# Attention into two feed-forward layers into routed experts: a two-byte search product and reshaped sums in the routing search, one product in place of two in the late second layer, and new step delays

## Chip, cores and metric

One core of one Trainium2 chip runs the whole program. The metric is the device time of one execution in microseconds. The engines are PE (matrix products), PEld (its weight loads), DVE and POOL (elementwise work and reductions; POOL also issues the indirect transfers), ACT (copies and activations) and SP (transfers). "Product" below means one matrix instruction on PE.

## What is computed

The reference, cut down:

```python
# attention over 32 memory slots per head: 8 batches, 8 heads, 576 positions, width 64
x = attn_out.transpose(0, 2, 1, 3).reshape(4608, 512)
# first feed-forward part: d_model 512, d_ff 768
h = np.maximum(np.maximum(x @ w1, x @ w2), x @ w3)
x = h @ w_out
# routed experts: 8 experts, cap = 4608 / 8 = 576 tokens each
logits = x @ w_gate
for idx in np.argsort(-logits.flatten()):      # greedy: best pair (token, expert) first
    tok, e = idx // 8, idx % 8
    if assigned[tok] >= 0 or counts[e] >= cap: continue
    assigned[tok] = e; counts[e] += 1
out[assigned == e] = np.maximum(x[assigned == e] @ w1[e], 0) @ w2[e]   # for each e
```

All inputs are float32, and the kernel keeps nearly full accuracy: each large product is done as three products of split operands (high by high, high by low, low by high).

## The kernel before, in words

The tokens are worked in four units of two batches (u = 0 to 3), nine tiles of 128 tokens each. For a unit the kernel does the attention, folds its result into the weights of the first layer (`fold`), runs the first layer (`layer1`, products of 288 columns) and the second (`layer2`). `layer2` makes 512 outputs and 8 gate logits at once: `w_out` has the product `w_out @ w_gate` set behind it as columns 512 to 519 (tiles `woh`, `wol`), so that a tile of 128 tokens takes 6 x 3 pairs of products of 260 columns. For the last two units the gate logits come ahead of the second layer, by `last_logits` (products of the whole hidden layer with the small matrix `wpp`, collected in `sc`, then `last_logits2`: copy, transposes, copy to `L`), and the last 15 of the 18 second-layer tiles of these units run after all logits are known. They are the first cover of the routing search.

The greedy assignment is done in eight phases (`ph`), one expert becoming full in each. A phase is a search for the threshold at which an expert is full, over the bits of the float, with 3 or 31 candidates at a time:

- `choose`: each token's best open expert (`OH`, 128 x 36 x 8) and its value `me`; then `reach` (which candidates each token reaches).
- seven rounds of `count` (nine products of `reach` with `OH` on PE, then five small DVE instructions that end in `some`) and `digit` (one product of `some` with `number` on PE that broadcasts the digit found, then DVE makes the next candidates `kj` and the next `reach`).
- after the last digit `cuts`: how many tokens of each expert lie above the threshold and at it, per partition (`part`).
- `close`: a product sums `part` over the partitions; DVE finds the expert that is full and updates the state. `ties` and `places` each start with a product of `before` with `lastb`; `places2` (four times) builds selection matrices `P1`, and `index` (36 products) turns them into the token list `gi`, `si` of the expert.

POOL then gathers the 576 token rows (`xg`, five indirect transfers), PE transposes them (`tr`, L974), and the expert runs its first layer (`l1`, 192 products of 288 columns) and its second (`l2`, 96 products of 512 columns for four tiles and 16 for the last 64 tokens). POOL splits the next expert's weights into low parts meanwhile (`al`, L985; `bl`, L995), and scatters the results.

The order of all this on the in-order engines is fixed when the program is written out. `Flow` keeps a queue of search steps, each with a delay; `flow.main` writes out a unit of main work (three or so products) and first pops queued steps that are due. The delay of a step is how much main work, in planned microseconds, stands between it and the next step. If a step's input is not ready when PE comes to its product, PE waits and everything behind waits too. Just before the fourth tile of `l2` (tile index t = 3) `ready(ph+1)` pops, without main work between, whatever is still queued up to the next token list, and issues its gather.

Of the kernel before, what the change touches and what calls it, by code (L numbers as in the profile page):

```python
# [142 lines left out]
def moe_kernel(tc, q, k, v, phi, w1, w2, w3, w_out, w_gate, m_w1, m_w2, out):  # L143
# [16 lines left out]
    with ExitStack() as ctx:  # L160
# [487 lines left out]
        def layer2(u, t, c, j):  # L648
            if c == 0 and j == 0:
                st["ps"] = [pp.tile([128, NA], F32, name="acc", bufs=3),  # L650
                            pp.tile([128, NA], F32, **(dict(name="fold", bufs=2) if t % 2 else dict(name="acc", bufs=3)))]
            ps = st["ps"]
            n = hs.index((u, t, c)) + 2
# [12 lines left out]
            if i < NF - 1:  # L666
                return
            xs = wp.tile([128, DM], F32, name="xs", bufs=2)
            A.activation(xs[:, :NA], ps[0], AF.Copy)
            A.activation(xs[:, NA:], ps[1][:, :DM - NA], AF.Copy)  # L670
            if u < NU - 2:
                V.tensor_copy(L[:, u * NT + t], ps[1][:, DM - NA:])
            (SP if u >= NU - 2 else A).dma_start(x2s[u * TU + t * 128:u * TU + t * 128 + 128, :], xs)

        def last_logits(u, i):

            if i == 0:
                st["ll", u] = pp.tile([128, TU // 3], F32, name="sc", bufs=1)
            for c in range(3):
                PE.matmul(st["ll", u][32 * c:32 * c + E], wpp[:, i],  # L680
                          st["hT", u][:, i, TU // 3 * c:TU // 3 * (c + 1)], start=(i == 0), stop=(i == NF - 1))

        def last_logits2(u):
            ll = st["ll", u]
            x = wp.tile([128, DM], F32, name="xs", bufs=2)[:, :TU // 3]
            V.memset(x, 0.0)
            for c in range(3):
                A.activation(x[32 * c:32 * c + E], ll[32 * c:32 * c + E], AF.Copy)
            p = pp.tile([128, 3, 128], F32, name="tr", bufs=2)
# [14 lines left out]
        def choose(ph):  # L704

            src = L if ph == 0 else Lm
            if ph:
                ecap = small([128, E], "ecap")
                V.tensor_scalar(ecap, st["oh", ph - 1], -2.0, 1.0, op0=OP.mult, op1=OP.add)
                V.tensor_scalar(ecap, ecap, FMAX, None, op0=OP.mult)  # L710
                V.tensor_tensor(Lm, L if ph == 1 else Lm, br(ecap, NC), op=OP.min)
                src = Lm
                V.tensor_scalar(ucap, asg, 0.0, None, op0=OP.is_ge)
                V.tensor_scalar(ucap, ucap, -2.0, 1.0, op0=OP.mult, op1=OP.add)
                V.tensor_scalar(ucap, ucap, FMAX, None, op0=OP.mult)
# [3 lines left out]
            eq = small([128, NC, E], "eq", bufs=1)  # L719
            V.tensor_tensor(eq, src, bc(m, E), op=OP.is_equal)  # L720
            V.tensor_tensor(eq, eq, br(em8, NC), op=OP.mult)
# [12 lines left out]
        def search_steps(ph, DD):  # L734
# [18 lines left out]
            def digit(n):  # L753
# [3 lines left out]
                PE.matmul(p, some.to_broadcast([32, 128]), number[:, 1 - nj // J:2 - nj // J], start=True, stop=True)  # L757
# [51 lines left out]
        def finish_steps(ph, DD):  # L809
            last = ph == E - 1  # L810

            def close():
# [10 lines left out]
                else:  # L823
# [12 lines left out]
                    st["oh", ph] = oh  # L836
# [14 lines left out]

                    V.scalar_tensor_tensor(remR, oh, 1e6, remR, op0=OP.mult, op1=OP.add)
# [31 lines left out]
            def places():  # L884
# [10 lines left out]
                V.tensor_scalar(hi, pi, 7, None, op0=OP.arith_shift_right)  # L895
                eh = small([128, NC, 5], "eh", bufs=1)
# [4 lines left out]
                st["P1"] = lo, R, []  # L901
# [153 lines left out]
        def main1(u, i, n, w):  # L1055
            last = u == NU - 1
            layer1(u, i, n // 2, n % 2, w)
            at = (0, 6)
            if u and 3 * n + w in at and i + 1 < NF:
                fold(u, i + 1, at.index(3 * n + w))  # L1060
            if last and w == 1 and n == 1 and i:
                last_logits(u, i - 1)
            if not last and i == NF - 1 and n > 1 and w == 0:
                split_h(*hs[u * NT * NF // 3 + n - 2])


        before = onesb = row = lanef = vals = em8 = me8 = thr0 = rowi = OH = reach = some = number = part = remR = asg = ucap = sign = zero = Lm = am8 = me = rp = None

        def consts():
            nonlocal before, onesb, row, lanef, vals, em8, me8, thr0, rowi, OH, reach, some, number, part, remR, asg, ucap, sign, zero, Lm, am8, me, rp  # L1070
# [12 lines left out]
            later.G.iota(row, pattern=[[1, 128]], base=0, channel_multiplier=0, allow_small_or_imprecise_dtypes=True)  # L1083
            rowi = rp.tile([128, J], I32, name="rowi")
# [30 lines left out]
            later.V.tensor_scalar(em8, row[:, :E], -float(E), None, op0=OP.add)  # L1115
            me8 = rp.tile([128, E], F32, name="me8")
# [9 lines left out]
            some = rp.tile([32, 1], F32, name="some")  # L1126
            later.V.memset(some, 1.0)

            number = rp.tile([32, 2], F32, name="number")
            big = rp.tile([32, 1], F32, name="big")  # L1130
            later.V.tensor_scalar(big, lanef[:32], float(J), 2.0 ** 23, op0=OP.is_equal, op1=OP.mult)
            for n, x in enumerate((J, 3)):
                later.V.scalar_tensor_tensor(number[:, n:n + 1], lanef[:32], float(x), big, op0=OP.is_lt, op1=OP.add)
# [17 lines left out]
        for u in range(NU):  # L1151
# [50 lines left out]
            if u == NU - 2:  # L1202
                attention.close()
                hp = pool("last", side="right")
                for i in range(NF):
                    last_logits(u, i)
                last_logits2(u)
# [4 lines left out]
        for ph in range(E):  # L1212
            DD = DELAYS[SETS[ph]]
# [14 lines left out]
        flow.early()  # L1228
        flow.due = flow.now
        spacer = rp.tile([1, 1], F32, name="spacer")  # L1230
        for u, t, c in hs[((NU - 2) * NT + 3) * NF // 3:]:
            for j in range(3):
                flow.main(lambda: layer2(u, t, c, j), 0.67)
# [67 lines left out]
```

## Time and profile before

| | |
|---|---|
| three timed runs | 1162.79, 1162.80, 1165.26 us (median 1162.8) |
| profiled execution | 1156.12 us, of which the span from first to last instruction is 1154.3 us |
| busy share of the span | PE 92%, PEld 81%, DVE 63%, ACT 34%, POOL 29% |
| mean granted clock of PE | 0.977 |

Products on PE are pipelined: the duration of one is longer than the step from one start to the next, so the rate is read from start to start.

### The profile page before, as it was taken

What the parts mean: (1) busy time and instruction counts of PE and PEld (TensorE: products, weight loads), DVE (VectorE), ACT (ScalarE), POOL (GpSimd) and SP (SyncE); (2) the same over time, 40 slices, a digit from 0 to 9 for tenths busy, and PEclk for the clock granted to TensorE, in tenths of its full rate; (3) what the DMA queues carried; (4) which work ended last, traced back from release to release, by engine and by line L of the source; (5) the groups of instructions that cost most, each with busy time, mean ns of one, the idle gap of its engine ahead of it and who ended that gap; (6) DMA issues with size and microseconds to landing.
All of it is one profiled execution on the core that took longest, in us unless ns stands there. A gap on an engine that the chain in (4) does not pass through costs nothing.

```text
span 1154.3 us, 22040 instructions
## 1 busy us (share of the span) xinstructions
PE 1067.4 (92%) x8743; PEld 931.2 (81%) x8743; DVE 721.9 (63%) x1767; ACT 398.0 (34%) x897; POOL 338.2 (29%) x362
## 2 busy tenths in 40 slices
PE   4698999989999999999997899898999999899996
PEld 3577799878998889778997788778788887879895
DVE  6798843774646446344686577879787887862120
ACT  2454434433343243322332313324142332424240
POOL 2123210120101101000001444555544455556552
PEclk8899999999999999999998989999999999999999
DMA  9964535336322430210132232333313232334311
GB/s 286 324 199 141 183 115 167 108 96 199 104 83 70 138 97 24 74 42 1 47 128 69 83 106 87 110 101 111 114 61 112 82 118 92 121 104 128 106 55 41
DMA packets 103767, 127.80 MB, mean 111 GB/s; under 512 B 18928, under 2 KB 79344, under 8 KB 103664
## 3 DMA queue, kind: packets, MB, share of 16 engines
q1 hardware_dynamic: 95184, 102.80, 28.9%
q0 software_dynamic: 5888, 18.88, 5.2%
q10 hardware_dynamic: 2592, 4.72, 1.1%
q8 instruction: 69, 1.13, 0.4%
q14 instruction: 34, 0.28, 0.1%
HBM read 102.78 MB, written 23.59 MB: 109 GB/s over the span
## 4 chain that ended last, share of the span: by engine, by line
PE 43%; DVE 10%; issue 3%; POOL 2%; ACT 1%; DMA 0%; POOLq 0%
PE acc L1033 13%; PE acc L1010 12%; PE acc L602 5%; PE acc L664 4%; PE acc L1037 2%; PE tr L974 1%; DVE reach L731 1%; PE fold L757 1%; DVE eq L798 1%; PE fold L664 1%; DVE hT L1013 1%; PE fold L743 1%; DVE part L800 1%; POOL bl L995 1%; DVE kn L787 1%
## 5 line engine op out<-in xcount | busy, mean ns | idle before, releaser
L602 PE MATMUL acc<-ah,Wh 128*128 128x288 f32 x576 | 180.1, 313 | 4.9 <-DVE hT L608 3.6
L602 PE MATMUL acc<-ah,Wl 128*128 128x288 f32 x576 | 169.8, 295 | 1.2 <-DVE Wl L586 1.2
L602 PE MATMUL acc<-al,Wh 128*128 128x288 f32 x576 | 169.9, 295 | 0.0
L1033 PE MATMUL acc<-bh,hT 128*128 128x512 f32 x512 | 168.4, 399 | 0.0
L1010 PE MATMUL acc<-woh,ah 128*128 128x288 f32 x512 | 161.0, 314 | 1.7 <-ACT woh L976 1.2
L1010 PE MATMUL acc<-wol,ah 128*128 128x288 f32 x512 | 154.9, 303 | 0.2
L1010 PE MATMUL acc<-woh,al 128*128 128x288 f32 x512 | 154.1, 301 | 0.0
L602 PEld LDWEIGHTS acc<-ah,Wh 128*128 128x128 f32 x576 | 108.2, 188 | 33.3 <-issue 13.9
L608 DVE TENSOR_TENSOR hT<-hT,acc 128x288 f32<-128x288 f32 x192 | 85.9, 450 | 75.1 <-PE acc L602 69.0
L1033 PEld LDWEIGHTS acc<-bh,hT 128*128 128x128 f32 x512 | 96.1, 188 | 21.3
L602 PEld LDWEIGHTS acc<-ah,Wl 128*128 128x128 f32 x576 | 108.2, 188 | 1.4 <-DVE Wl L586 1.4
L602 PEld LDWEIGHTS acc<-al,Wh 128*128 128x128 f32 x576 | 108.4, 188 | 0.1
L985 POOL TENSOR_TENSOR al<-wa,ah 128x512 fp32r<-128x512 f32 x64 | 82.8, 1300 | 72.4 <-ACT ah L984 72.0
L1010 PEld LDWEIGHTS acc<-woh,ah 128*128 128x128 f32 x512 | 99.6, 195 | 3.2 <-ACT woh L976 1.7
L1012 ACT ACTIVATE hT<-acc 128x288 fp32r<-128x288 f32 x128 | 52.6, 411 | 142.4 <-PE acc L1010 136.4
L1033 PE MATMUL acc<-bl,hT 128*128 128x512 f32 x256 | 100.5, 392 | 0.0
L1010 PEld LDWEIGHTS acc<-wol,ah 128*128 128x128 f32 x512 | 99.5, 194 | 1.0 <-DVE wol L977 0.7
L1010 PEld LDWEIGHTS acc<-woh,al 128*128 128x128 f32 x512 | 99.6, 195 | 0.0
L962 POOL DMA_INDIRECT xg<-x2s,gi x40 | 39.3, 982 | 191.9 <-DVE some L751 172.7
L995 POOL TENSOR_TENSOR bl<-wa,bh 128x512 fp32r<-128x512 f32 x64 | 83.6, 1322 | 24.3 <-ACT bh L994 24.0
L1013 DVE SCALAR_TENSOR_TENSOR hT<-acc,hT 128x288 fp32r<-128x288 f32 x128 | 56.2, 452 | 52.4 <-ACT hT L1012 51.7
L606 ACT ACTIVATE hT<-acc 128x288 f32<-128x288 f32 x96 | 38.9, 411 | 144.6 <-PE acc L602 142.6
(253 smaller groups left out, 2204.9 us busy)
## 6 DMA issues: line engine op xcount, KB each, us to landing
wa<-in_moe_w_dram SPq DMA_DIRECT2D x64, 512.0 KB, 3.7
wr<-ws SPq DMA_DIRECT2D x36, 384.0 KB, 3.1
dw<-in_moe_w_dram SPq DMA_DIRECT2D x36, 256.0 KB, 5.3
q<-in_q_dram SPq DMA_DIRECT2D x7, 1024.0 KB, 5.9
kv<-in_k_dram SPq DMA_DIRECT2D x27, 256.0 KB, 4.1
kv<-in_v_dram SPq DMA_DIRECT2D x27, 256.0 KB, 4.9
ws<-wr SPq DMA_DIRECT2D x12, 384.0 KB, 3.1
x2s<-xs ACTq DMA_DIRECT2D x18, 256.0 KB, 2.0
```

The costliest lines, as they stand in the source:

```text
L602: PE.matmul(p, x[:, b, g, f], y[:, g, c], start=(n == 0), stop=(n == 5))
L606: A.activation(o, p, AF.Copy)
L608: V.tensor_tensor(o, o, p, op=OP.max)
L664: PE.matmul(ps[a], x[:, j], y[:, i, NA * a:NA * a + NA], start=(i == 0 and m == 0), stop=(i == NF - 1 and m == 2))
L962: G.indirect_dma_start(out=x[:n], out_offset=None, in_=x2s, in_offset=bass.IndirectOffsetOnAxis(ap=gi[:n, t:t + 1], axis=0))
L985: G.tensor_tensor(lo, r, hi.bitcast(F32), op=OP.subtract)
L995: G.tensor_tensor(lo, r, hi.bitcast(F32), op=OP.subtract)
L1010: PE.matmul(p, x[:, k], y[:, k, c], start=(k == 0 and i == 0), stop=(k == 3 and i == 2))
L1012: A.activation(hh[:, m, c], p, AF.Relu)
L1013: V.scalar_tensor_tensor(hl[:, m, c], p, 0.0, hh[:, m, c].bitcast(F32), op0=OP.max, op1=OP.subtract)
L1033: PE.matmul(p, x[:, m, c], y[:, m], start=(m == 0 and i == 0), stop=(m == K - 1 and i == 2))
L1037: PE.matmul(p, st["hx", m // 4][:, m % 4], y[:, m], start=(m == 0 and y is bh), stop=(m == K - 1 and y is bl))
```

## The change

It does eight things. (1) The digit's product takes two-byte operands and swaps their places: `number`, widened to 32 x 128 in bf16, becomes the loaded weight, and `some`, now bf16, the moving column. (2) `cuts` makes the signed flags `gs` in bf16, each doubled (last axis of 2, from `me` and the threshold at once), multiplies them with `OH` in bf16 into one tile `gx` for both thresholds, and sums that in one reduction; the float flags `ge` are made behind it. (3) `P1` is built from a doubled bf16 list `lod` and a bf16 row `rowb`. (4) `choose` uses a bf16 `em8b`; `ecap` is computed in `close` of the phase before, and `ucap` in two instructions in place of three. (5) `layer2` of the last two units drops the gate columns: one product of 512 columns in place of two of 260, one PSUM tile and one copy. (6) The logits of unit 2 are taken group by group inside unit 3's first layer, and collected in a `tr` tile. (7) The transposes of unit 3's logits come behind the first third of a late tile. (8) One set of delays replaces the two used in turn.

```diff
-DELAYS = ((4.38, 1.21, 1.9, 2.85, 3.39, 2.06, 2.18, 1.4, 1.31),
-          (3.53, 1.14, 2.24, 3, 3.11, 2.54, 2.15, 1.3, 1.62),
-          (3.33, 0.04, 2.75, 3.0, 3.09, 1.99, 2.38, 1.18, 1.41))
-SETS = (1, 0, 1, 0, 1, 0, 1, 0)
+DELAYS = (4.0, 1.3, 2.25, 4.2, 3.2, 3.5, 2.15, 0.9, 1.3)
...
-                for a in range(2):
-                    PE.matmul(ps[a], x[:, j], y[:, i, NA * a:NA * a + NA],
+                for a, p in enumerate(ps):
+                    PE.matmul(p, x[:, j], y[:, i, width * a:width * a + width],
...
-                PE.matmul(p, some.to_broadcast([32, 128]), number[:, 1 - nj // J:2 - nj // J], start=True, stop=True)
+                PE.matmul(p, number[:, 1 - nj // J], some, start=True, stop=True)
...
             def cuts(ph, t):
+                gs = small([128, 2, NC, 2], "gs", BF, bufs=1)
+                for j, op in enumerate((OP.is_gt, OP.is_ge)):
+                    V.scalar_tensor_tensor(gs[:, j], bc(me, 2), t, bc(sign, 2), op0=op, op1=OP.mult)
+                x = small([128, 2, NC, E], "gx", BF, bufs=1)
+                for j in range(2):
+                    V.tensor_tensor(x[:, j].rearrange("p c (k a) -> p c k a", a=2),
+                                    OH.rearrange("p c (k a) -> p c k a", a=2),
+                                    gs[:, j].unsqueeze(2).to_broadcast([128, NC, E // 2, 2]), op=OP.mult)
+                with nc.allow_low_precision("counts up to 36"):
+                    V.tensor_reduce(part, x.rearrange("p j c e -> p j e c"), axis=AX.X, op=OP.add)
                 ge = small([128, 2, NC], "ge", bufs=1)
                 V.tensor_scalar(ge[:, 0], me, t, None, op0=OP.is_gt)
                 V.tensor_scalar(ge[:, 1], me, t, None, op0=OP.is_ge)
-                gs = small([128, 2, NC], "gs", bufs=1)
-                V.tensor_tensor(gs, ge, br(sign, 2), op=OP.mult)
-                x = small([128, NC, E], "eq", bufs=1)
-                for j in range(2):
-                    V.tensor_tensor(x, OH, bc(gs[:, j], E), op=OP.mult)
-                    with nc.allow_low_precision("counts up to 36"):
-                        V.tensor_reduce(part[:, j], x.rearrange("p c e -> p e c"), axis=AX.X, op=OP.add)
...
-                V.tensor_tensor(x, bc(lo[:, NC // 4 * n:NC // 4 * (n + 1)], 128), br(row, NC // 4), op=OP.is_equal)
+                V.tensor_tensor(x.rearrange("p c (k a) -> p c k a", a=2),
+                                lo[:, NC // 4 * n:NC // 4 * (n + 1)].unsqueeze(2).to_broadcast([128, NC // 4, 64, 2]),
+                                rowb.rearrange("p (k a) -> p k a", a=2).unsqueeze(1).to_broadcast([128, NC // 4, 64, 2]),
+                                op=OP.is_equal)
...
+            if last and w == 1:
+                if n == 1 and i:
+                    last_logits(u, i - 1)
+                if n == 3 and i + 1 < NF:
+                    last_logits(u - 1, i)
...
+        for j in range(3):
+            layer2(*late[0], j)
+        last_logits3(NU - 1)
```

Three places show how the rows on the engines change. First PE in a late second-layer tile, around one digit of the first search phase (`acc` and `fold` are PSUM tiles, `hh` and `hl` the split hidden layer); before:

```order
L664 MATMUL acc<-woh,hh 128x260
L664 MATMUL fold<-woh,hh 128x260
L664 MATMUL acc<-wol,hh 128x260
L664 MATMUL fold<-wol,hh 128x260
L664 MATMUL acc<-woh,hl 128x260
L664 MATMUL fold<-woh,hl 128x260
L757 MATMUL fold<-number,some 128x1
L664 MATMUL acc<-woh,hh 128x260
```

And the same place now:

```order
L666 MATMUL acc<-woh,hh 128x512
L666 MATMUL acc<-wol,hh 128x512
L666 MATMUL acc<-woh,hl 128x512
L759 LDWEIGHTS number
L759 MATMUL fold<-some,number 128x1
L666 MATMUL acc<-woh,hh 128x512
```

Six products became three wider ones, and the digit has a weight load of its own that does not depend on `some`.

Second DVE, from the last digit of the second search phase to the start of its `close` (`hT` is the expert's hidden layer, not part of the search); before:

```order
L776 TENSOR_TENSOR fb<-fold,fbx 128x1
L792 TENSOR_SCALAR ge<-me,fb 128x36
L793 TENSOR_SCALAR ge<-me,fb 128x36
L795 TENSOR_TENSOR gs<-ge,sign 128x72
L798 TENSOR_TENSOR eq<-OH,gs 128x288
L800 TENSOR_REDUCE part<-eq 128x8
L798 TENSOR_TENSOR eq<-OH,gs 128x288
L800 TENSOR_REDUCE part<-eq 128x8
L1013 SCALAR_TENSOR_TENSOR hT<-acc,hT 128x288 x3
L828 TENSOR_TENSOR full<-fold,remR 128x8
```

And now:

```order
L778 TENSOR_TENSOR fb<-fold,fbx 128x1
L796 SCALAR_TENSOR_TENSOR gs<-me,fb,sign 128x72 x2
L799 TENSOR_TENSOR gx<-OH,gs 128x288 x2
L803 TENSOR_REDUCE part<-gx 128x16
L805 TENSOR_SCALAR ge<-me,fb 128x36
L806 TENSOR_SCALAR ge<-me,fb 128x36
L1027 SCALAR_TENSOR_TENSOR hT<-acc,hT 128x288 x2
L834 TENSOR_TENSOR full<-fold,remR 128x8
```

Five instructions stand between `fb` and the end of `part` where seven stood, and the two `ge` moved behind it.

Third POOL, in the first expert's second layer, from its first scatter (`out_dram`) to the next expert's first weight splits; before:

```order
L1044 MEMSET spacer 1x1
L1045 DMA out_dram<-o,si 4608x512
L1020 COPY xs<-hT 128x4x64 x2
L962 DMA xg<-x2s,gi 128x512 x4
L962 DMA xg<-x2s,gi 64x512
L1044 MEMSET spacer 1x1
L1045 DMA out_dram<-o,si 4608x512
L1020 COPY xs<-hT 128x4x64 x2
L1044 MEMSET spacer 1x1
L1045 DMA out_dram<-o,si 4608x512
L985 TENSOR_TENSOR al<-wa,ah 128x512 x2
```

And now:

```order
L1058 MEMSET spacer 1x1
L1059 DMA out_dram<-o,si 4608x512
L1034 COPY xs<-hT 128x4x64 x2
L1058 MEMSET spacer 1x1
L1059 DMA out_dram<-o,si 4608x512
L1034 COPY xs<-hT 128x4x64 x2
L1058 MEMSET spacer 1x1
L1059 DMA out_dram<-o,si 4608x512
L976 DMA xg<-x2s,gi 128x512 x4
L976 DMA xg<-x2s,gi 64x512
L999 TENSOR_TENSOR al<-wa,ah 128x512 x2
```

The gather of the next expert's tokens stood behind the first scatter and now stands behind the third, directly ahead of the splits.

## Rows read from the trace of the kernel before

**Rows 1.** Page: span and busy time by engine.

```profile
span 1154.3 us, 22040 instructions
...
PE 1067.4 (92%) x8743; PEld 931.2 (81%) x8743; DVE 721.9 (63%) x1767; ACT 398.0 (34%) x897; POOL 338.2 (29%) x362
```

**Rows 2.** Chain that ended last: start us, us, engine, tile and line, products.

```profile
599.42 4.45 PE acc L664 x37
...
665.54 6.74 PE acc L1010 x30
...
774.46 1.19 PE acc L1010 x9
...
865.60 4.98 PE acc L1010 x24
...
932.78 5.62 PE acc L1010 x30
...
974.73 0.80 PE acc L1010 x6
...
1038.68 25.56 PE acc L1010 x192
1064.24 22.19 PE acc L1033 x96
...
1092.86 11.92 PE acc L1010 x90
```

**Rows 3.** Waits of PE, 634 to 1040 us: who for whom, us, times, longest.

```profile
PE fold L825 <- DVE part L800: 15.4, 6, 4.4
PE fold L887 <- DVE lastb L879: 4.5, 4, 1.3
```

**Rows 4.** PE timeline around a digit (L757) and a `ties` product (L860).

```profile
711.00 0.29 PE L1010 MATMUL acc<-woh,al 128*128 128x288 f32 x1
711.23 0.38 PE L757 MATMUL fold<-number,some 32*128 32x1 f32 x2
...
711.77 0.30 PE L1010 MATMUL acc<-wol,ah 128*128 128x288 f32 x1
...
737.12 0.30 PE L1010 MATMUL acc<-woh,al 128*128 128x288 f32 x1
737.25 0.18 PE L860 MATMUL fold<-lastb,before 128*128 128x1 bf16 x1
...
737.50 0.30 PE L1010 MATMUL acc<-wol,ah 128*128 128x288 f32 x1
```

**Rows 5.** DVE timeline, first and last instruction of `cuts`, second phase.

```profile
727.87 1.20 DVE L792 TENSOR_SCALAR ge<-me,fb 128x36 f32<-128x36 f32 x1
...
732.45 0.67 DVE L800 TENSOR_REDUCE part<-eq 128x8 bf16<-128x288 f32 x1
```

**Rows 6.** DVE timeline, the same two instructions, first phase.

```profile
586.89 0.24 DVE L792 TENSOR_SCALAR ge<-me,fb 128x36 f32<-128x36 f32 x1
...
589.34 0.74 DVE L800 TENSOR_REDUCE part<-eq 128x8 bf16<-128x288 f32 x1
```

**Rows 7.** POOL timeline over the start of rows 5.

```profile
726.49 2.54 POOL L995 TENSOR_TENSOR bl<-wa,bh 128x512 fp32r<-128x512 f32 x2
```

**Rows 8.** Window after a wait: us, busy of PE, PEld, DVE, ACT, POOL, granted clock, DMA.

```profile
665.40:670.40 5.00, 5.00 (x22) 5.00 (x23) 3.29 (x20) 0.93 (x2) 1.28 (x1) 0.50 0.29 92
```

**Rows 9.** PE timeline at the last logits of units 2 and 3.

```profile
473.28 0.47 PE L691 MATMUL tr<-ident,xs 96*128 96x96 f32 x3 [1.62 <-ACT xs L688]
...
548.75 0.47 PE L691 MATMUL tr<-ident,xs 96*128 96x96 f32 x3 [1.55 <-ACT xs L688]
```

**Rows 10.** DVE group of `P1`: busy us, mean ns, idle before.

```profile
L906 DVE TENSOR_TENSOR P<-lo,row 128x1152 bf16<-128x1152 int32 x32 | 41.8, 1362 | 0.0
```

**Rows 11.** Page: gather's issue (busy us, mean ns) and us to landing.

```profile
L962 POOL DMA_INDIRECT xg<-x2s,gi x40 | 39.3, 982 | 191.9 <-DVE some L751 172.7
...
xg<-x2s,gi POOLq DMA_INDIRECT x40, 3.6
```

More of the change, by code (lines that the diff above doesn't have):

```diff
@@ L648, in layer2 @@
         def layer2(u, t, c, j):
+            late = u >= NU - 2
             if c == 0 and j == 0:
-                st["ps"] = [pp.tile([128, NA], F32, name="acc", bufs=3),
-                            pp.tile([128, NA], F32, **(dict(name="fold", bufs=2) if t % 2 else dict(name="acc", bufs=3)))]
+                if late:
+                    st["ps"] = [pp.tile([128, DM], F32, name="acc", bufs=3)]
+                else:
+                    st["ps"] = [pp.tile([128, NA], F32, name="acc", bufs=3),
+                                pp.tile([128, NA], F32, **(dict(name="fold", bufs=2) if t % 2 else dict(name="acc", bufs=3)))]
             ps = st["ps"]
+            width = DM if late else NA
             n = hs.index((u, t, c)) + 2
@@ L707, in choose @@
             if ph:
[L708 to L711, printed above, removed]
+                V.tensor_tensor(Lm, L if ph == 1 else Lm, br(st["ecap", ph - 1], NC), op=OP.min)
                 src = Lm
-                V.tensor_scalar(ucap, asg, 0.0, None, op0=OP.is_ge)
-                V.tensor_scalar(ucap, ucap, -2.0, 1.0, op0=OP.mult, op1=OP.add)
-                V.tensor_scalar(ucap, ucap, FMAX, None, op0=OP.mult)
+                V.tensor_scalar(ucap, asg, 0.0, -2.0, op0=OP.is_ge, op1=OP.mult)
+                V.tensor_scalar(ucap, ucap, 1.0, FMAX, op0=OP.add, op1=OP.mult)
             m = small([128, NC], "m")
@@ L718, in choose @@
             V.tensor_tensor(me, m, ucap, op=OP.min)
[L719 removed]
+            eq = small([128, NC, E], "eq", BF, bufs=1)
             V.tensor_tensor(eq, src, bc(m, E), op=OP.is_equal)
[L721 removed]
+            V.tensor_tensor(eq, eq, br(em8b, NC), op=OP.mult)
             V.tensor_reduce(am8, eq, axis=AX.X, op=OP.min)
@@ L850, in close @@
                     st["tie"] = tie, sc, lb, kk, amE, es
+                    ecap = st["ecap", ph] = small([128, E], "ecap")
+                    V.tensor_scalar(ecap, oh, -2.0, 1.0, op0=OP.mult, op1=OP.add)
+                    V.tensor_scalar(ecap, ecap, FMAX, None, op0=OP.mult)
                     V.scalar_tensor_tensor(remR, oh, 1e6, remR, op0=OP.mult, op1=OP.add)
@@ L1060, in main1 @@
                 fold(u, i + 1, at.index(3 * n + w))
-            if last and w == 1 and n == 1 and i:
-                last_logits(u, i - 1)
+            if last and w == 1:
[3 more added lines that the diff above has]
+                    last_logits(u - 1, i)
+                if i + 1 == NF and n in (0, 2, 3):
+                    (lambda u: last_logits(u, NF - 1), None, last_logits2, last_logits3)[n](u - 1)
             if not last and i == NF - 1 and n > 1 and w == 0:
                 split_h(*hs[u * NT * NF // 3 + n - 2])
-        before = onesb = row = lanef = vals = em8 = me8 = thr0 = rowi = OH = reach = some = number = part = remR = asg = ucap = sign = zero = Lm = am8 = me = rp = None
+        before = onesb = row = rowb = lanef = vals = em8 = em8b = me8 = thr0 = rowi = OH = reach = some = number = part = remR = asg = ucap = sign = zero = Lm = am8 = me = rp = None
         def consts():
-            nonlocal before, onesb, row, lanef, vals, em8, me8, thr0, rowi, OH, reach, some, number, part, remR, asg, ucap, sign, zero, Lm, am8, me, rp
+            nonlocal before, onesb, row, rowb, lanef, vals, em8, em8b, me8, thr0, rowi, OH, reach, some, number, part, remR, asg, ucap, sign, zero, Lm, am8, me, rp
             unit0.close()
@@ L1083, in consts @@
             later.G.iota(row, pattern=[[1, 128]], base=0, channel_multiplier=0, allow_small_or_imprecise_dtypes=True)
+            rowb = rp.tile([128, 128], BF, name="rowb")
+            later.V.tensor_copy(rowb, row)
             rowi = rp.tile([128, J], I32, name="rowi")
@@ L1115, in consts @@
             later.V.tensor_scalar(em8, row[:, :E], -float(E), None, op0=OP.add)
+            em8b = rp.tile([128, E], BF, name="em8b")
+            later.V.tensor_copy(em8b, em8)
             me8 = rp.tile([128, E], F32, name="me8")
@@ L1125, in consts @@
             later.V.memset(reach, 0.0)
-            some = rp.tile([32, 1], F32, name="some")
+            some = rp.tile([32, 1], BF, name="some")
             later.V.memset(some, 1.0)
-            number = rp.tile([32, 2], F32, name="number")
+            number = rp.tile([32, 2, 128], BF, name="number")
             big = rp.tile([32, 1], F32, name="big")
@@ L1132, in consts @@
             for n, x in enumerate((J, 3)):
-                later.V.scalar_tensor_tensor(number[:, n:n + 1], lanef[:32], float(x), big, op0=OP.is_lt, op1=OP.add)
+                later.V.scalar_tensor_tensor(number[:, n], lanef[:32].to_broadcast([32, 128]), float(x),
+                                             big.to_broadcast([32, 128]), op0=OP.is_lt, op1=OP.add)
             part = rp.tile([128, 2, E], BF, name="part")
@@ L1228, in moe_kernel @@
         flow.early()
+        spacer = rp.tile([1, 1], F32, name="spacer")
+        late = hs[((NU - 2) * NT + 3) * NF // 3:]
+        for j in range(3):
+            layer2(*late[0], j)
+        last_logits3(NU - 1)
         flow.due = flow.now
-        spacer = rp.tile([1, 1], F32, name="spacer")
-        for u, t, c in hs[((NU - 2) * NT + 3) * NF // 3:]:
+        for u, t, c in late[1:]:
             for j in range(3):
```

23 lines of the change are left out of this document (12 added, 11 removed).

## The prediction

> **What bounds the kernel now.** I read the page first: PE is busy 92% of the 1154.3 us span [rows 1], so a saving counts only if it shortens PE's own row of products or a wait in it. Then I followed the chain that ended last. From the seventh expert on it is PE alone: that expert has no search beside it, and takes from 1038.68 to 1092.86, 54.2 us [rows 2]. Experts three to five, with a search each, start at 774.46 and the sixth starts at 974.73: 66.8 us apiece [rows 2]. So a search costs an expert 12.6 us though PE's search products are tiny. Last I read PE's waits over the six experts with a search: 15.4 us in six waits for `part` at the `close` product, and 4.5 us in four for `lastb` at the `places` product [rows 3]. The rest is PE work of the search: digits above all (below).
>
> **Change by parts, against the profiled execution.**
>
> *Digit.* From the start of the product ahead to that of the second product behind, a digit takes 711.77 - 711.00 = 0.77 us; `ties`, which has the form the digit gets (two-byte operands, one moving column), takes 737.50 - 737.12 = 0.38 between like neighbours [rows 4]. Without inserted work two products of 288 columns take 2 x 0.133 (25.56 / 192 [rows 2]) = 0.27. So a digit falls from 0.50 to 0.11 or 0.12. There are 7 in each of 7 searches: 49 x 0.38 = **-18.6 us**. It is on PE's path in all of them but the two or three between the late layer and the first gather. Bounds: 0, if `some` ended last at every digit (PE mostly comes to it without a wait: the digit of rows 4 shows none), and -24, if the weight load, which no longer waits, also shortens the waits there are.
>
> *Cuts and their delay.* In the second phase `cuts` runs from 727.87 to 733.12, 5.25 us [rows 5]; in the first, where POOL is idle, from 586.89 to 590.08, 3.19 us [rows 6]. The difference is DVE being held: the first `ge` takes 1.20 us against 0.24, and ends at 729.07 where POOL's instruction ends at 729.03 [rows 5, 6, 7]. The new chain has two `gs`, two `gx`, one reduction of 576 elements. Estimates from rows: `gs` like `ge`, 0.24 each; `gx` at most half of a 1.36 us `P1` row scaled by 288 / 1152 plus a fixed 0.15, so 0.3 to 0.46; the reduction at most twice 0.74 [rows 6, 10]. Sum 2.6 to 2.9 us free of POOL. PE's cover between the last digit and `close` was 24 to 27 products of 288 columns (3.2 to 3.6 us); counted in the new order it is 15 of 288 and 12 of 512 columns in phases three to seven, 15 x 0.133 + 12 x 0.231 (22.19 / 96) = 4.8 us [rows 2], 21 and 9 in the second. One hold of 1 us is then covered, two nearly. Half of it lies in `l2`, where POOL splits nothing for the first three tiles. I leave 0.25 us a phase: **-14 us** of the 15.4 [rows 3], bounds -4 (as many holds as now) and -15.4.
>
> *What the wait does to the clock.* After the longest wait, five microseconds ran at a granted clock of 0.50, that is 1.2 GHz, with 22 products in them [rows 8]. Three pieces of the chain are such: 30 products in 6.74 us, 24 in 4.98, 30 in 5.62, against 0.133 each: 2.7 + 1.8 + 1.6 = **-6 us** [rows 2] if the waits shrink as above, 0 if they stay.
>
> *Places.* 18 to 21 products of 288 columns (2.4 to 2.8 us) stood between `ties` and `places`; now 18 of 512, 4.2 us, and behind the end of POOL's splits. The four waits go: **-4.5 us** [rows 3]; 0 at worst. What is late next is `ties`: its cover falls from 27 or more products (3.6 us) to 15 wide ones (3.5), with two `ge` and two `hT` now ahead of `full` on DVE; I charge 0.3 a phase, **+2 us**. `ecap`, moved behind `lastb`, holds only `lim`, which has the 4.2 us. `P1`, even at 1.36 us [rows 10], is covered but for about 1 us by the 27 wide products (6.2 us) ahead of `index`.
>
> *Late second layer.* 37 products of 260 columns step 0.120, a pair 0.241; one of 512 steps 0.231 [rows 2]. 18 tiles x 18 pairs x 0.0095 = **-3 us**. The search beside it still fits: six narrow products became three wide ones, and `some` is ready sooner than both.
>
> *Last logits.* The wait of 1.55 at unit 3 goes, **-1.6 us**; at unit 2 the 1.62 goes too [rows 9], but six groups of float32 products are now set singly between split ones, and a float32 step so set costs up to the digit's 0.50. I take zero there (+1.5 to -1.6).
>
> *Gather.* Counted in the order, `index` now falls exactly at the fourth tile in every phase, where the queue is popped in any case; before it came 24 to 30 wide products earlier. The gather stands behind the third scatter on POOL. From there: about 2 us to its start, then five issues of 0.98 + 0.3, the last landing 3.6 us after its issue [rows 11]: tokens at 5.6 to 10.8 us. PE's first transposes come after `index` (1 us) and 28 wide products, 7.5 to 8 us, the fifth near 12. It fits by 1 to 2 us. I charge **+1 us** in all; bounds 0 and +10.
>
> Sum: -18.6 - 14 - 6 - 4.5 + 2 - 3 - 1.6 + 1 = -44.7. Check by stages: an expert that takes 66.8 us with its search becomes 66.8 - 7 x 0.38 - (14 + 6 + 4.5) / 6 + 0.5 = 60.5 us; six of them save 38, and the late layer's seven digits, its products and the last logits add 2.6 + 3 + 1.6: 45 us. The charges on ties and gather look high rather than low, so I take **-46.5 us**: 1156.1 becomes about 1109.6. The three timed runs lie 6.7 us above the profiled execution; I put the same saving under their median: 1162.8 - 46.5 = **1116 us**.
>
> **The Trainium skill against the trace.** The row shows one DVE instruction held until POOL's end [rows 5, 7]. "SBUF — State Buffer", section "SBUF: two separate sides", says that DVE instructions with two SBUF inputs and GpSimd share a port pair under an exclusive lock, so that the loser blocks for the whole instruction. By that rule all four of `gs` and `gx` can each lose, as the old ones could; that is the second case below. "VectorE: DVE Perf Modes", section "The perf-mode tier table", gives `tensor_tensor` in bf16 twice the rate and `tensor_reduce` none; by it `gx` would be 0.3 and the reduction not faster per element, which is inside my bounds. No row before shows an all-bf16 `tensor_tensor`.
>
> **Rivals.** (a) *The waits at `close` stay.* If each of four two-input instructions is held by POOL for up to 1.2 us, `cuts` takes 2.9 + 4.8 = 7.7 against 4.8: the close wait stays near 2.5 us and with it part of the cold clock. For: holds of a whole POOL instruction are seen. Against: at most two or three per `cuts` now, and POOL's splits end with `l1`. Then -46.5 + 14 + 4 = -28: 1134 us. (b) *Late tokens.* If the gather starts 3 us later than I reckon, PE waits 2 to 3 us before six experts, +15: 1131 us. (c) *Slower.* The same place decides: with no cover left the search ends just at the gather, and every late microsecond is paid six times. It eats the whole gain when the wait reaches 46.5 / 6 = 7.8 us per expert, say from DVE running the next `choose` and `reach` ahead of the transposed tokens' low parts; at 9 us it is 1170. (d) *The digit is not on the path:* only covers and clock gain, -25, 1138 us. (e) *All waits vanish* and the digit gives its bound: -54, 1109 us.
>
> **Numbers.** Forecast (within 9 us) 0.66, (a) 0.13, (b) 0.07, (d) 0.04, (e) 0.06, (c) 0.03, no measurable change 0.01. A change within 0.2% (2.3 us) cannot be told from none here. Faster 0.96, same 0.01, slower 0.03. The forecast's own range is 1109 to 1125; to hold 8 in 10 it takes in (e) and most of (a) and (b): 1106 to 1134.
>
> **What would show it.** Right: digits at one product and no long step behind; `close` waits under 0.5 us; no stretch at clock 0.50 between experts; expert starts 59 to 61 us apart; late products at 0.231. Wrong: PE waiting for `part` or `lastb` as before, for `xg` or the low parts `wol` at the transposes, or `gx` rows over 1 us.

## The result and the profile after

The changed kernel takes 1129.93 us (median of four runs, 1128.45 to 1131.02) against 1163.18 beside it: a ratio of 0.971, interval 0.9693 to 0.9727. That is 33 us faster, where 46.5 were forecast: inside the stated range, outside the forecast's own (1109 to 1125).

The two profiled executions differ by 1154.3 - 1126.7 = 27.6 us. The rest of the 33 is scatter: runs of the kernel before lay between 1155.2 and 1167.9 over all its measurements, and its profiled one at 1156.1. In one program part that is the same in most kernels here, up to the last logits, the traced executions differ by up to 7 us. So terms are compared stage by stage below; only the balance at the end is set beside the two spans.

First the chain that ended last (start us, us, engine, tile and line, products) and PE's waits, 632 to 1012 us (who for whom, us, times, longest), of the changed kernel. They answer to [rows 2] and [rows 3].

```profile
742.36 0.91 PE fold L927 x36
...
931.64 0.91 PE fold L927 x36
```

```profile
PE tr L988 <- DVE wol L991: 8.1, 6, 1.6
PE fold L759 <- DVE some L753: 5.0, 10, 0.7
PE fold L759 <- issue: 0.8, 1, 0.8
PE fold L831 <- DVE part L803: 0.7, 1, 0.7
```

An expert with a search is 63.1 us long, from `index` to `index` (three of them between the two lines), where [rows 2] had 66.8 and I expected 60.5. From the first expert's first product to the seventh's, six experts with a search took 402.0 us before and take 380.3 now:

```profile
636.49 0.61 PE L1010 MATMUL acc<-woh,ah 128*128 128x288 f32 x1 [0.69 <-ACT woh L976]
...
1038.52 0.29 PE L1010 MATMUL acc<-woh,ah 128*128 128x288 f32 x1
```

```profile
628.54 0.61 PE L1024 MATMUL acc<-woh,ah 128*128 128x288 f32 x1 [0.69 <-ACT woh L990]
...
1008.85 0.40 PE L1024 MATMUL acc<-woh,ah 128*128 128x288 f32 x1
```

That is 21.7 us for the six, where the prediction's check by stages had 38; the parts ahead of them gave 8.0, where it had 7.2; behind them 2.0 were lost. The shortfall lies in the experts. The wait for `part` is gone but for the first expert, the wait for `lastb` altogether. But two have come: before the transposes of tokens (`tr`) for low parts (`wol`), and before digits for `some`. In the kernel before these read, 634 to 1040 us:

```profile
PE fold L757 <- DVE some L751: 1.6, 7, 0.3
...
PE tr L974 <- DVE wol L977: 1.1, 3, 0.4
```

The digit, on PE's timeline:

```profile
765.08 0.29 PE L1024 MATMUL acc<-woh,al 128*128 128x288 f32 x1
765.30 0.17 PE L759 MATMUL fold<-some,number 32*128 32x1 bf16 x1
765.41 0.40 PE L1024 MATMUL acc<-woh,ah 128*128 128x288 f32 x1
765.64 0.30 PE L1024 MATMUL acc<-wol,ah 128*128 128x288 f32 x1
```

From the product ahead to the second behind it is 765.64 - 765.08 = 0.56 us. Less two steps of 0.133 the digit costs 0.30, as the other digits without a wait do (median 0.30): less than the 0.50 of [rows 4], but more than twice a `ties` product.

Then `cuts` on DVE, in the late layer, where POOL is idle, and in a later phase, where POOL works (start us, us, line, tiles, shapes; x2 is two instructions in one row):

```profile
583.74 0.50 DVE L796 SCALAR_TENSOR_TENSOR gs<-me,fb,sign 128x72 bf16<-128x72 f32 x2
584.15 0.52 DVE L799 TENSOR_TENSOR gx<-OH,gs 128x288 bf16<-128x288 bf16 x2
584.71 1.18 DVE L803 TENSOR_REDUCE part<-gx 128x16 bf16<-128x576 bf16 x1
...
786.38 1.45 DVE L796 SCALAR_TENSOR_TENSOR gs<-me,fb,sign 128x72 bf16<-128x72 f32 x2
787.75 1.61 DVE L799 TENSOR_TENSOR gx<-OH,gs 128x288 bf16<-128x288 bf16 x2
...
789.40 1.18 DVE L803 TENSOR_REDUCE part<-gx 128x16 bf16<-128x576 bf16 x1
```

Alone the chain takes 2.2 us, beside POOL 4.2, against a cover of 4.8: two of its four instructions are held there. The granted clock (the column after POOL's) of ten microseconds behind three waits of the kernel before at `close`:

```profile
662.00:672.00 10.00, 6.65 (x31) 6.66 (x31) 7.04 (x25) 1.86 (x4) 3.73 (x4) 0.66 0.43 147
862.00:872.00 10.00, 8.07 (x49) 7.67 (x48) 8.07 (x28) 3.63 (x8) 6.51 (x6) 0.83 0.43 138
931.00:941.00 10.00, 8.40 (x52) 8.26 (x53) 8.24 (x33) 3.24 (x8) 5.56 (x5) 0.83 0.42 137
```

And of the changed kernel, behind two `close` products and behind a wait for `wol`:

```profile
662.00:672.00 10.00, 9.35 (x44) 6.91 (x42) 6.87 (x33) 0.60 (x1) 2.22 (x6) 1.00 0.36 110
726.00:736.00 10.00, 10.00 (x46) 7.60 (x45) 6.66 (x32) 0.60 (x1) 1.88 (x6) 1.00 0.44 126
941.00:951.00 10.00, 8.28 (x52) 6.59 (x51) 6.56 (x18) 3.99 (x8) 4.70 (x7) 0.83 0.34 100
```

The granted clock stays at 1.00 (2.4 GHz) behind `close`, where [rows 8] had 0.50. It still falls once among the experts, behind the wait for `wol` at 945.38.

And the new wait for `wol`, on DVE and PE:

```profile
752.65 0.69 DVE L991 TENSOR_TENSOR wol<-tr,woh 128x512 fp32r<-128x512 f32 x1 [2.64 <-ACT woh L990]
...
754.04 1.32 DVE L733 TENSOR_TENSOR reach<-me,kj 128x1116 bf16<-128x1116 f32 x1
...
755.38 1.28 DVE L991 TENSOR_TENSOR wol<-tr,woh 128x512 fp32r<-128x512 f32 x2
...
756.12 0.66 PE L988 MATMUL tr<-ident,xg 128*128 128x128 f32 x4 [1.60 <-DVE wol L991]
```

The first digit, `reach` with it, stands between the low parts of the first two token tiles. The PSUM tile `tr` has two buffers, so the fourth transposes wait for the second low part: 1.60 us in four experts alike, 1.08 and 0.58 in two others.

### The profile page after: what moved, and what is told of

Read it like the earlier page. It is cut to its first block, busy times and chain, and to the rows that moved or that the text cites. A ratio compares the mean times of both kernels' runs of the same rounds, so it can differ in the third digit from the quotient of the medians.

```text
span 1126.7 us, 21277 instructions
## 1 busy us (share of the span) xinstructions
PE 1049.9 (93%) x8370; PEld 893.1 (79%) x8370; DVE 688.4 (61%) x1773; ACT 395.1 (35%) x879; POOL 346.1 (31%) x362
## 3 DMA queue, kind: packets, MB, share of 16 engines
q8 instruction: 66, 1.08, 0.4%
## 4 chain that ended last, share of the span: by engine, by line
PE 40%; DVE 5%; issue 3%; POOL 2%; ACT 1%; DMA 0%; POOLq 0%; DVEq 0%
PE acc L1024 15%; PE acc L1047 14%; PE acc L666 6%; DVE reach L733 2%; PE tr L988 1%; PE acc L1051 1%; PE fold L745 1%; DVE wol L991 1%; PE fold L759 1%; POOL bl L1009 1%; PE fold L927 1%; ACT woh L990 1%; POOL out_dram L1059 0%; DVE hT L1027 0%; DMA xg<-x2s,gi 0%
## 5 line engine op out<-in xcount | busy, mean ns | idle before, releaser
L599 PEld LDWEIGHTS acc<-ah,Wh 128*128 128x128 f32 x576 | 108.1, 188 | 39.5 <-issue 15.4
L1024 PEld LDWEIGHTS acc<-woh,ah 128*128 128x128 f32 x512 | 97.2, 190 | 7.9 <-ACT hT L1026 5.3
L1009 POOL TENSOR_TENSOR bl<-wa,bh 128x512 fp32r<-128x512 f32 x64 | 92.2, 1469 | 1.9 <-ACT bh L1008 1.9
L434 POOL TENSOR_TENSOR at<-at,ssm 128x512 f32<-128x512 f32 (+1 forms) x20 | 21.2, 1060 | 216.5 <-DVE ssm L432 172.9
```

Source lines behind the costliest of these rows:

```text
L434: G.tensor_tensor(at, at, sm.unsqueeze(2).to_broadcast([n, 2 * H, M]), op=OP.mult)
L599: PE.matmul(p, x[:, b, g, f], y[:, g, c], start=(n == 0), stop=(n == 5))
L1009: G.tensor_tensor(lo, r, hi.bitcast(F32), op=OP.subtract)
L1024: PE.matmul(p, x[:, k], y[:, k, c], start=(k == 0 and i == 0), stop=(k == 3 and i == 2))
```

## The experiments

My theory after the result: the changed kernel lost its missing 13 us or so to two things, the digit's price (0.30 for 0.12) and the stretch from `index` to the next first layer, where tokens and the first digit now meet on DVE. The rivals: the shorter instructions alone did it, the delays alone did it, and every wait is POOL holding DVE. Each ratio is to the kernel before, timed beside it on the same chip. PE's waits of these runs are read from 600 us on; so they take in the stretch ahead of the first expert, where the changed kernel too waits twice 1.0 us for `some` and once 1.6 us at a count.

**The digit on 128 rows.** `number` is zero in the added rows.

```diff
-            some = rp.tile([32, 1], BF, name="some")
+            some = rp.tile([128, 1], BF, name="some")
-            number = rp.tile([32, 2, 128], BF, name="number")
+            number = rp.tile([128, 2, 128], BF, name="number")
```

> The changed kernel with one edit: `some`, `number` and `big` get 128 partitions in place of 32, the added rows of `number` being zero, so that the digit's product has the 128 rows of the products around it. In the changed kernel an unstalled digit costs 0.30 us, `ties` 0.13. Theory A (a 32-row product between 128-row products costs 0.17 more): digits fall to 0.12 to 0.14, and 49 of them save about 8 us: 1121 to 1123 us. Rival B (the 0.30 is the digit's wait for `some` or a fixed price of a product whose weight load follows a wait): digits stay at 0.30 and the time at 1128 to 1131.

```profile
769.00 0.30 PE L1024 MATMUL acc<-woh,al 128*128 128x288 f32 x1
769.14 0.18 PE L759 MATMUL fold<-some,number 128*128 128x1 bf16 x1
769.18 0.38 PE L1024 MATMUL acc<-woh,ah 128*128 128x288 f32 x1
769.39 0.30 PE L1024 MATMUL acc<-wol,ah 128*128 128x288 f32 x1
```

Now 769.39 - 769.00 = 0.39, less 0.27: 0.12 us. So the price is the number of rows, and theory A holds for the product. The time is 1126.13 us, ratio 0.9677 (0.9654 to 0.97): 4 us under the changed kernel, not 8, and the two intervals just overlap. Unstalled digits gain 0.17 each; those that wait for `some` need not, and the transposes wait 1.4 us longer in all. What else the other 4 us went into is not shown.

**The old digit in the changed kernel.** 
```diff
-                PE.matmul(p, number[:, 1 - nj // J], some, start=True, stop=True)
+                PE.matmul(p, some.to_broadcast([32, 128]), number[:, 1 - nj // J:2 - nj // J], start=True, stop=True)
```

> The changed kernel with the old float32 digit (some widened as the weights, number as one moving column). Theory A (every digit is on PE's path and the change took 0.20 us from each): +9.8 us, 1138 to 1141. Rival (in the new order the digit's product is hidden, or stands where PE waits anyway): no change, 1128 to 1131.

1136.51 us, ratio 0.9762 (0.9733 to 0.9792): 6.6 us more than the changed kernel, below the 9.8 of 49 digits by 0.20, and between the two expectations. That part of the difference falls into waits that are there anyway is my reading; no run shows it.

**The old delays in the changed kernel.**

```diff
-            DD = DELAYS
+            DD = DELAYS[SETS[ph]]
```

> The changed kernel with the old three sets of delays. Theory A (the step order is what took the waits at `close` and `places` away, since `cuts` in the first layer is held by POOL as before and takes over 5 us): `close` waits of 1.5 to 3 us come back in most phases, `places` waits of 1 us too; the waits for low parts (`wol`, 1.6 us five times) and for `some` go: 1138 to 1148. Rival (the shorter `cuts` took them away, and the new delays only brought the new waits): no `close` wait over 0.5 us, time 1115 to 1122.

1161.07 us, ratio 0.9974 (0.9955 to 0.9993): slower than either theory said, and hardly faster than before. All of the change but the delays is worth 0.3% in the old order. PE's waits, and the rows of `cuts` in four phases (the last numbers: busy us, mean ns, idle before):

```profile
PE fold L834 <- DVE part L806: 18.0, 6, 3.2
```

```profile
L802 DVE TENSOR_TENSOR gx<-OH,gs 128x288 bf16<-128x288 bf16 x8 | 10.7, 1379 | 0.0
L799 DVE SCALAR_TENSOR_TENSOR gs<-me,fb,sign 128x72 bf16<-128x72 f32 x8 | 9.6, 1243 | 0.1
L806 DVE TENSOR_REDUCE part<-gx 128x16 bf16<-128x576 bf16 x4 | 4.7, 1166 | 0.1
```

Two `gs`, two `gx` and the sum make 2 x 1.24 + 2 x 1.38 + 1.17 = 6.4 us: in the first layer the new chain is slower than the old one's 5.25 [rows 5], each of its four instructions being more than four times its free length (0.29 for `gs`, 0.30 for `gx`). The other waits did not go as theory A had it either: over the experts PE waits 6.3 us for `wol`, up to 3.0 at once, and 6.7 for `reach`. The granted clock over the six experts is 0.95, where it was 0.98 in the kernel before.

**The old `cuts` in the changed kernel.** The removed lines of `cuts` in place of the added ones:

```diff
-                gs = small([128, 2, NC, 2], "gs", BF, bufs=1)
...
+                gs = small([128, 2, NC], "gs", bufs=1)
+                V.tensor_tensor(gs, ge, br(sign, 2), op=OP.mult)
...
```

> The changed kernel with the old float chain in `cuts` (ge, gs, two products with two sums). Theory A (place and cover, not the shorter chain, removed the waits at `close`): `cuts` takes 3.2 to 3.6 us in the second layer, under its cover of 4.8; only the first expert's wait grows; 1129 to 1132. Rival (the shorter chain is needed): `close` waits of 0.5 to 2 us in all phases, 1133 to 1142.

1136.11 us, ratio 0.9758 (0.9733 to 0.9784): the rival's size, at its lower end. PE's waits:

```profile
PE fold L828 <- DVE part L803: 3.4, 6, 1.6
```

The first expert waits 1.6 us, the others some 0.4 each. So most of the 15.4 us is gone by the place alone, and the shorter chain takes the last 2.7 (3.4 less 0.7). The rest of the 6 us lies where the traces do not tell it from scatter.

**The new delays alone, in the kernel before.**

```diff
-            DD = DELAYS[SETS[ph]]
+            DD = DELAYS
```

> The kernel before with one edit: the new set of delays in all phases. Theory A (the order of the search steps is the largest part of the change by itself, and the shorter instructions add 10 to 16 us): no `close` wait over 1 us behind the first expert, no `places` wait, the waits for `wol` come, digits stay at 0.50: 1142 to 1149 us. Rival (the new order needs the shorter instructions; with the old ones it waits at `close`, at `index` and at the digits): 1154 to 1163.

1146.05 us, ratio 0.9891 (0.9869 to 0.9914), 12.4 us under its own base of 1158.47 and inside theory A's range. By ratios the delays alone give 1.1%, the rest alone 0.3%, both 2.9%. The new waits come with the delays: 3.7 us for `wol` and 4.2 for `some` over the experts, where the kernel before had 1.1 and 1.6. What the old instructions still wait for:

```profile
PE fold L911 <- DVE P L904: 4.2, 5, 0.8
...
PE fold L823 <- DVE part L798: 1.6, 5, 0.3
```

`index` waits 0.8 us for a `P1` of 1.46 us on average: the prediction's "covered but for about 1 us". In the changed kernel a `P1` takes 0.75 to 0.95 and that wait does not exist.

**The first digit ahead of the transposes.** 
```diff
-            steps.append((lambda: (choose(ph), above(thr0)), DD[0]))
+            steps.append((lambda: (choose(ph), above(thr0)), 3.5 if ph else DD[0]))
-                steps.append((lambda n=n: count(n), DD[1]))
+                steps.append((lambda n=n: count(n), 1.5 if ph and not n else DD[1]))
```

> The changed kernel with the first two delays of a search (phases two to seven) set so that the first digit stands ahead of the first token transposes and not behind them. Theory A (the 1.6 us that PE waits for `wol` once per expert are the `reach` of that digit, which DVE runs between the low parts of tokens): these waits go, 8 to 10 us with what hangs on them: 1119 to 1123. Rival (DVE is short of time in that stretch whatever the order, and the wait moves to the second count or digit): 1127 to 1131.

1136.17 us, ratio 0.981 (0.9792 to 0.9829): 1% worse than the changed kernel, and slower than both expectations. Waits, and one DVE instruction with POOL's row beside it:

```profile
PE tr L988 <- DVE wol L991: 10.9, 5, 2.2
PE fold L745 <- DVE fb L776: 5.2, 6, 1.6
```

```profile
753.09 2.84 DVE L768 TENSOR_TENSOR fb<-fb,sm 128x1 int32<-128x1 int32 x1
```

```profile
753.37 2.54 POOL L999 TENSOR_TENSOR al<-wa,ah 128x512 fp32r<-128x512 f32 x2
```

An instruction of one element per row takes 2.84 us, in five experts alike, and ends at 755.93, where POOL's two subtractions end (755.91). By the profile it starts 0.28 us ahead of the first of them; the trace does not show what kept it from ending in that time. They are the next expert's first `al`, and start when POOL's last gather issue is out. In the changed kernel DVE waits for ACT at that moment, so nothing shows. The waits for `wol` grew where theory A had them go. That is no proof against its cause for them, since the edit moved a wait under a hold.

**Early digit and 128 rows,** the two edits above together.

> The digit on 128 rows and the early first digit together. Theory A (two separate prices): 12 us or more under the changed kernel: 1113 to 1118. Rival (the digits' 0.17 us only lengthen waits for DVE, so that they do not add up): not under e6 by more than 2 us.

1136.47 us, ratio 0.9817 (0.9797 to 0.9838): nothing gained over the run before, as the rival said. The waits for `wol` are 11.9 us here, against 10.9: where DVE is late, a cheaper product on PE only waits longer.

**No subtraction on POOL, old delays.** A memset in place of `al` and `bl`; the low parts of the experts' weights are left out of the result.

```diff
-            G.tensor_tensor(lo, r, hi.bitcast(F32), op=OP.subtract)
+            G.memset(lo.bitcast(F32), 0.0)
```

> The changed kernel with the old delays, and with POOL's subtraction that makes the low parts of the expert weights replaced by a memset to zero (the low parts of the experts' weights are left out of the result; the products on PE stay). To be compared with the run with the old delays. Theory A (DVE's `gs` and `gx` at 1.3 us each are held by POOL's subtractions): they fall to 0.26 us, `cuts` to 2.2 to 2.6, `close` waits under 0.7, `reach` to 1.32: 1130 to 1142. Rival (DVE is late at `cuts` for its own work, or through another engine): `close` waits of 1.5 to 3 us stay, 1155 or more.

1113.08 us, ratio 0.961 (0.959 to 0.9631), against 0.9974 with the subtraction: 3.6%, some 42 us, is the price of the holds in the old order. It is more than theory A said. DVE's rows:

```profile
L736 DVE TENSOR_TENSOR reach<-me,kj 128x1116 bf16<-128x1116 f32 x28 | 37.2, 1328 | 1.0
...
L802 DVE TENSOR_TENSOR gx<-OH,gs 128x288 bf16<-128x288 bf16 x10 | 2.6, 301 | 0.0
L799 DVE SCALAR_TENSOR_TENSOR gs<-me,fb,sign 128x72 bf16<-128x72 f32 x10 | 2.5, 291 | 0.2
```

`gs` falls from 1.24 to 0.29 us, `gx` from 1.38 to 0.30, `reach` from 1.59 to 1.33; no wait for `part` is left among PE's. The granted clock over the six experts rises from 0.95 to 0.99, so a part of the 42 us is clock behind the waits. The memset also shortens POOL's own work (122 us busy in the six experts for 203); no run separates that, but PE waits for POOL in neither of the two. The Trainium skill, "SBUF — State Buffer", section "SBUF: two separate sides", states the lock on a DVE instruction with two SBUF inputs only against a GpSimd instruction that reads SBUF; a memset reads none, and the trace agrees.

**The same edit with the new delays.**

> The changed kernel, its own delays, with POOL's subtraction replaced by a memset to zero (low parts of the experts' weights left out). With the old delays the same edit gave a ratio of 0.961 to the kernel before. Theory A (the new delays are worth their 2.6% only because they put `cuts` where POOL holds DVE less; without holds the two orders are about equal): ratio 0.953 to 0.967. Rival (the new order is better in itself, by its longer covers): 0.948 or less. Either way no `gs` or `gx` row over 0.4 us; the wait of 1.6 us for `wol`, which comes from an unheld `reach`, stays.

1131.99 us, ratio 0.9732 (0.9706 to 0.9757): both expected ratios wrong. Without holds the new order is no faster than with them, and 1.2% slower than the old order without them.

```profile
PE tr L988 <- DVE wol L991: 7.3, 5, 1.6
...
PE fold L759 <- DVE some L753: 4.1, 5, 1.0
```

```profile
758.00:763.00 5.00, 4.09 (x24) 3.32 (x25) 3.46 (x9) 2.07 (x4) 0.44 (x1) 0.54 0.00 0
763.00:768.00 5.00, 5.00 (x31) 4.64 (x31) 3.00 (x10) 1.34 (x3) 1.54 (x3) 0.78 0.12 28
```

The waits for `wol` stay, as expected, since they come from an unheld `reach`, and behind one of them the clock is at 0.54 and 0.78 for ten microseconds. Over the experts PE waits 16 us in this run, at transposes and digits, and 2 us with the old delays. So the new order dodges the holds, and pays for it there.

**Low parts of the expert weights on DVE.** The subtraction is written two groups of products later, on DVE; with the digit on 128 rows; the second of the two has the old delays.

```diff
-            G.tensor_tensor(lo, r, hi.bitcast(F32), op=OP.subtract)
-            done(j)
+            late_lo.append([2, lambda: V.tensor_tensor(lo, r, hi.bitcast(F32), op=OP.subtract), lambda: done(j)])
```

> The changed kernel with the digit on 128 rows, and the subtractions for the low parts of the expert weights done by DVE, two products' groups later, in place of POOL; nothing is left out. 16 of them per expert at 0.69 us (the price of the same form in `wol`) are 11 us of DVE work, against some 7 us of holds that go. Theory A (holds cost more than the work, since they fall on waits of PE): ratio 0.955 to 0.968, all waits at `close` below 0.3. Rival (DVE becomes the bound, the work stands in the search's chains): ratio 0.975 or more, waits for `some` and `reach` at most digits.

> The same as the run before it, with the old three sets of delays. Theory A (without holds the old order is no worse): within 0.006 of the ratio of the same kernel with the new delays. Rival (the old order's shorter covers, 3.6 us at `close`, don't hold 2.2 us of `cuts` and one or two subtractions of 0.69): above it by 0.01 or more, with waits at `close` again.

Ratios 0.9734 (0.9711 to 0.9757; 1132.62 us) and, with the old delays, 0.9796 (0.9773 to 0.9819; 1139.44 us). With the new delays:

```profile
PE fold L759 <- DVE some L753: 16.9, 16, 1.9
```

No wait at `close` is left, but digits wait for `some` (14.8 of these us among the experts): the rival's mechanism, at a size between the two, and 0.6% above the same kernel with POOL's subtraction (0.9677). The second pair's difference of 0.006 is the edge of its theory A, and decides nothing.

**Only the first two low parts on DVE,** with the early digit and 128 rows.

```diff
-                    if more_ and (t, m) in ((3, 2), (3, 6)):
-                        split1(ph + 1, m // 4)
+                    if more_ and (t, m) in ((3, 2), (3, 4)):
+                        split1(ph + 1, m // 2 - 1)
-            G.tensor_tensor(lo, r, hi.bitcast(F32), op=OP.subtract)
+            (V if ph and m < 2 else G).tensor_tensor(lo, r, hi.bitcast(F32), op=OP.subtract)
```

> The early first digit and the digit on 128 rows, and POOL's first two subtractions for the next expert (from the second expert on) moved to DVE, behind `reach` of the first count, where DVE waits 1 to 2 us for that count. Nothing is left out. Theory A (the early first digit failed only because these two, which start when POOL's gathers end, hold a DVE instruction of one element per row for 2.8 us): that row falls to 0.16 us, the wait for `wol` (2.2 us an expert) goes, experts are 60 to 61.5 us apart and the ratio is 0.955 to 0.964. Rival (the stretch from `index` to the first layer is short of time on DVE whatever POOL does): waits of over 1 us at the transposes stay, ratio 0.968 or more.

```profile
754.94 0.16 DVE L768 TENSOR_TENSOR fb<-fb,sm 128x1 int32<-128x1 int32 x1
```

```profile
PE fold L745 <- DVE fb L776: 4.2, 9, 0.7
...
PE fold L745 <- DVE reach L733: 3.1, 3, 1.6
...
PE tr L988 <- DVE wol L991: 1.1, 2, 0.7
```

The held instruction is 0.16 us again, and the wait for `wol` falls from 11.9 to 1.1: theory A's mechanism. The ratio is 0.9666 (0.9646 to 0.9687; 1125.81 us), short of its 0.955 to 0.964. Among the experts PE now waits 4.2 us for `fb` and 0.7 for `reach` at the counts (the rest of `reach` is ahead of the first expert), and the two subtractions are 2.6 us more of DVE's work per expert; what each takes back is not shown. It is 1.5% under the same kernel with both subtractions on POOL (0.9817), and the fastest complete version measured; from the digit on 128 rows alone (0.9677) it cannot be told apart. That kernel waits 8.2 us for `wol`; so taking the waits of the changed kernel's own order away gained nothing that these runs can tell.

## Why the prediction was right in direction and too large

The direction, the sign of each large term and the range held; the forecast itself did not. That the range held is in part luck: it was made wide for rivals (a) and (b), whose 1134 and 1131 lie close to the 1129.9 measured, and neither struck, as `close` hardly waits and no tokens were late behind the first expert. Two of the prediction's own signs of being wrong came true, the waits for `wol` and `gx` rows over 1 us (one of 1.39 to 1.40 in every expert), and two of being right did not: experts 59 to 61 us apart, and no stretch at clock 0.50. Point by point:

- *Digit*, -18.6: the mechanism was right, the size not. The step that failed is the comparison with `ties`: that product has 128 rows, the digit 32, and the digit costs 0.30, not 0.12. 49 x 0.20 = 9.8 us. The first experiment shows the cause. The Trainium skill, "TensorE: Matmul & The Clock Gate", section "Why this matters for your kernels", has a single product of 32 rows take the same time as one of 128; set between products of 128 rows it does not here (0.30 against 0.12).
- *Cuts*, -14: 15.4 us of waits became 0.7, so -14.7. The new place does it: in the old place the wait is 18.0 even with the new chain. My reading of holds was right ("one hold of 1 us is then covered, two nearly"), and so was rival (a)'s mechanism: in the first layer all four instructions are held, as its 7.7 us had it (6.4 measured). It did not strike since only two holds fall on the new place (three in the first expert, which still waits 0.7).
- *Clock*, -6: the windows behind `close` are at 1.00, as expected. The three windows of ten microseconds above lost 3.4 + 1.7 + 1.7 us of clock before, the one behind `wol` loses 1.7 now: about -5.
- *Places*, -4.5: gone. *Ties*, +2: no wait for `lastb` shows; the charge was not needed.
- *Late second layer*: from its first to its last product 69.2 us (546.1 to 615.3) against 74.8 (549.0 to 623.8) before. Of the 5.5 us some 2 are the search's (eight digits at 0.30 for nine at 0.50, and fewer counts), which leaves about 3, as forecast. *Last logits*, -1.6: the wait of [rows 9] at unit 3 is gone; what unit 2's spreading gives is below the scatter of that part.
- *Gather*, +1: the other step that failed. The tokens came in time behind the first expert, as worked out; what came late was DVE. I named that in rival (c) ("DVE running the next `choose` and `reach` ahead of the transposed tokens' low parts"), but gave it to a case of 0.03 and not to the sum. The waits for `wol` grew by 7.0 us (1.1 to 8.1) and those of the digits by 4.2 (1.6 to 5.0 + 0.8); of the latter 5.8 us, 3.6 stand at or just behind the transposes and 2.2 at other digits. With the digit's 8.8 this is the size of what is missing. Which of the two is larger is not shown: the run that took the `wol` waits away put others in their place.

The balance: -44.7, corrected by +8.8 for the digit, -0.7 for `close`, -2 for ties and +11.2 - 1 for the new waits, is -28.4, beside 27.6 between the two spans. So close a match is luck, as the spans scatter by more and some terms stand in it as forecast. The 1.8 us that the prediction added to its sum, as its charges on ties and gather looked high, went the wrong way for the gather.

Left open: why ACT begins the first token tile's high parts 1.4 us behind its transposes (752.02 against an end at 750.65), which brings the first `wol` late; and an order that keeps the old places with POOL's subtraction out of DVE's way and nothing left out, which was tried only in the one version with all of it on DVE (0.9796).

## What to carry to other kernels

When an instruction on another engine can be held, its place decides more than its length: the shortened chain took 2.7 us of waits away in its new place and none in its old one (18.0 against 15.4). When a change of order removes a wait, price the stretch into which the steps move by the engine that serves it, not only by the data that arrive there. And compare a product with one of its own shape in every dimension before its price is borrowed.

## What the runs showed of the hardware

- A product of 32 rows between products of 128 rows costs 0.30 us, the same with 128 rows (zeros in the added ones) 0.12.
- A DVE instruction of 128x1 was held for 2.84 us, over two POOL subtractions in a row, in five experts of five: it did not get its turn between them.
- Reductions were not held: 1.18 us with POOL idle, 1.17 in the first layer beside it. `gs`, at more than four times its free length, stands next to them in the same rows.
- The bf16 `gx`, 288 elements a row, took 0.30 us without holds (two in a row 0.52), the low end of the 0.30 to 0.46 estimated.
